# New list weights for the attention, a reordered start, and token gathers at another step of the ranked experts

## The chip, the core and the metric

The kernel runs on one core of a Trainium2 chip. The metric is the device time of one execution in microseconds (us). The core has a matrix engine (PE, whose weight loads are shown apart as PEld), a vector engine (DVE), an activation engine (ACT), a general engine (POOL) and a queue engine (SP) that only issues transfers. Each engine works through its own list of instructions in order; semaphores make one engine wait for another. Matrix products end up in PSUM banks; everything else lives in SBUF or in DRAM.

## The reference

Two stages follow each other. The first is causal attention with a decay, for 8 batches, 8 heads, 576 positions, head size 64:

```
scores = q k^T / 8 + cum[i] - cum[j],   cum = cumsum(log(clip(f, 1e-4, 1)))
attn   = softmax(scores, causal);       x = attn @ v      -> (8, 576, 512)
```

The second is a mixture of 8 experts with one expert for each token. A token takes the expert with the largest logit, or, where its local gate is at least 0.5, the expert of the token before it. Then

```
out[b, s] = p[e] * (relu(x[b, s] @ w1[e]) @ w2[e]),   w1: 512 x 1024, w2: 1024 x 512
```

The result has to be close to that of float32, so most operands are split into a high and a low half of 16 bits, and a product takes three matrix products of such halves.

## The kernel before, in words

**Attention (about 5 to 388 us of the span).** A batch is cut into 25 units of 512 score columns. A unit goes through these stages: scores on PE into a bank `st` (L905, with the mask added at L912), the negated row maximum on DVE (`nm`, L916), the exponential on ACT (`P`, L936), four transposes on PE into `pt` (L951), the high half on ACT (`ph`, L956), the low half on DVE (`pl`, L960), and the products with v on PE into `xp` (L930). For units named in `SUBS` the low half is made by PE and ACT in place of DVE (L963, L968). Beside that stand the turning of q and k for the next batch (L429, L438 to L442), the normalisation (L991, L995), and a side chain that computes the gate and the routing of earlier batches.

The order is written by a planner at build time. `issue()` keeps a clock for each engine and a queue for each stage, and takes the instruction with the smallest planned start plus a weight: `LEADS` has a weight for each stage and batch, `RANKS` settles ties, `SW` is the weight of the side chain, `GI` says after which unit a batch's gate is queued, `TS` and `TE` at which unit and on which engine (A for ACT, D for DVE) the turned groups of q and k are taken, `DUE` and `LATE` at which planned time the work of the first two batches is put in. The planned clock is not the chip's clock; the order it leaves is all that the chip sees.

**The start (`start()`).** Heads 0 to 2 of batch 0 are turned on PE (`heads`, L536) and get their decays by a small product with `spk` (`decays`, L541). `spk` comes from a chain: log on ACT (L278), a scan on DVE (L280), and casts and subtractions on DVE (`by_chunks`, `parts`, L287 to L300). `head_hi` and `head_b` (L554, L558) are ACT copies of a head, `head_lo` (L567, L569) is the low half on DVE.

**Experts (388 us to the end).** Experts 0 and 1 are done first; early parts of their tokens use `early_tok` (gathers by POOL at L1706, then transposes by SP at L1711). The other six are ranked by their number of tokens, rank r = 0 to 5. For each rank there are some 48 steps: steps 0 to 27 are `seven`, the first product by a scheme of seven half-size products (PE L1870, copies `et` on ACT at L1877, sums on DVE at L1883, relu on ACT L1887), and from step 28 on the second product `y`, four steps for each tile of 128 tokens (PE L1827, or L1831 for half a tile). A finished tile is scaled by ACT into `o` (L1763, L1798), and POOL writes it to its rows of the output (a scatter, L1766, L1799), behind a `drain` of POOL (L1773). There are three `o` buffers: the fourth `o` waits until the first one's scatter has landed.

What else a rank does is tied to its steps by a list, sorted by step: weight loads of the next rank by SP (four at step 0, one each at the steps in `UN` = 5, 24, 29), sums of weight quarters by POOL (`LA`, steps 6 to 13, L2154 to L2163), their halves by ACT and DVE (`WC`), and the tokens of rank r + 2: five gathers by POOL at step `XA[0]`, their transposes by SP at step `XA[1]`. A step is a place in the order, not a time: an instruction runs when its engine reaches it and its inputs are there.

Of the kernel before, what the change touches and what calls it, by code (L numbers as in the profile page):

```python
# [35 lines left out]
SUBS = ((7, 11, 14, 16), (7, 11, 14), (7, 11, 14, 16), (7, 11, 14, 16, 22), (7, 10, 11, 16), (7, 8, 11, 20), (2, 4, 11, 12, 14, 16), (7, 11, 13, 14, 21))  # L36


def moves_of(d):
# [17 lines left out]
GI = (21, 21, 16, 16, 16, 16, 11, 12)  # L57
SW = ((-700, 0, 0), (-700, 0, 0), (-700, 0, 0), (-700, 200, -200), (-700, 0, 0), (-700, 0, 0), (-700, 0, 0), (-800, 0, 0))
TS = ({'q': (13, 17, 18, 20, 20), 'k': (19, 20, 20, 21, 21)}, {'q': (13, 17, 18, 20, 20), 'k': (19, 20, 20, 21, 21)}, {'q': (13, 17, 18, 20, 20), 'k': (19, 20, 20, 21, 21)}, {'q': (13, 17, 18, 20, 20), 'k': (19, 20, 20, 21, 21)}, {'q': (13, 17, 18, 20, 20), 'k': (19, 20, 20, 21, 21)}, {'q': (13, 17, 18, 20, 20), 'k': (19, 20, 20, 21, 21)}, {'q': (13, 17, 18, 20, 22), 'k': (19, 20, 20, 21, 21)}, {'q': (12, 17, 18, 20, 20), 'k': (19, 20, 20, 21, 21)})
TE = ({'q': 'ADDDA', 'k': 'DAAAD'}, {'q': 'ADDDA', 'k': 'DAAAD'}, {'q': 'ADDDA', 'k': 'DAAAD'}, {'q': 'ADDDA', 'k': 'DAAAD'}, {'q': 'ADDDA', 'k': 'DAAAD'}, {'q': 'ADDDA', 'k': 'DAAAD'}, {'q': 'ADDDA', 'k': 'DAAAD'}, {'q': 'ADDDA', 'k': 'DAAAD'})  # L60
RANKS = (
# [8 lines left out]
)  # L70
LEADS = (
# [30 lines left out]
UC = (0, 0), (1, 1), (2, 2), (22, 23), (24, 25), (26, 27)  # L102
UB = 45
UN = (5, 24, 29)
XA = (32, 42)
# [11 lines left out]
def kernel(  # L117
# [138 lines left out]
    spm = cp.tile([64, 3, 512], F16, name="spm")  # L256
    spt = cp.tile([64, 3, 64], F16, name="spt")
    one = cp.tile([1, 1], F32, name="one")
    nc.vector.memset(one, 0.0)

    spk = cp.tile([97, 512], F16, name="spk")
    nc.vector.memset(spk, 0.0)
# [471 lines left out]
    def decays(h):  # L734
        for nm in "kq":
            add_decay(HS[h, nm], h, nm)
# [1939 lines left out]
```

## Time and profile before

| | |
|---|---|
| three runs | 777.99, 784.38 and 788.38 us; median 784.38 |
| profiled execution | 782.12 us, span of the instructions 780.3 us |
| PE busy | 733.5 us, 94% of the span |
| DVE, ACT, POOL busy | 598.4 (77%), 507.5 (65%), 467.3 us (60%) |
| DMA engines, mean busy share | 56.4% for the queue of SP's transfers, 8.1% for POOL's |
| granted PE clock | 1.00 in nearly all of the 40 slices, 0.995 on average |

The sums below are made against the profiled execution, which lies 2.3 us under the median of the three. PE's busy time counts each product up to a modelled end, so gaps of less than about 0.2 us between two products do not show as idle time. The idle time that an engine shows is followed by the name of what ended it, in square brackets.

### The profile page before, as it was taken

The page shows a single profiled execution, that of the slowest core. Times are in us where ns is not written, and L with a number is a line of the kernel's source. Part 1 is how long each engine was busy: PE and PEld are TensorE (multiplying, and loading weights), DVE is VectorE, ACT ScalarE, POOL GpSimd, SP SyncE. Part 2 cuts the span into 40 slices and gives each one's busy share as a digit, 9 for nine tenths or more (in the row PEclk, how much of TensorE's full clock was granted, in tenths as well). Part 3 has the DMA queues.
Part 4 walks back from the last instruction along what each step waited for, and adds up shares of the span by engine and source line. Part 5 has one row for each costly group of instructions (what it writes and reads, how often), then busy time and mean ns, then how long its engine had stood idle before and what let it go on. Part 6 is the DMA issues. An engine that isn't in the chain of part 4 may idle for free.

```text
span 780.3 us, 21918 instructions
## 1 busy us (share of the span) xinstructions
PE 733.5 (94%) x8661; PEld 533.4 (68%) x8661; DVE 598.4 (77%) x1295; ACT 507.5 (65%) x1006; POOL 467.3 (60%) x521
## 2 busy tenths in 40 slices
PE   5899999999999898988899999999999997999997
PEld 3687788788878777877655576675765655566683
DVE  7887788898998889899758847669596784868650
ACT  7898788888878878867643334456574644747441
POOL 5879989395689759838682464455371744434201
PEclk9999999999999999999999999999999998999999
DMA  7568979596976969156794766577658274651201
GB/s 177 146 132 176 167 181 187 132 194 162 182 175 128 178 162 179 38 102 197 179 272 149 221 138 142 149 210 162 212 139 233 78 161 181 169 206 56 82 3 51
DMA packets 189659, 120.75 MB, mean 155 GB/s; under 512 B 129397, under 2 KB 165511, under 8 KB 189532
## 3 DMA queue, kind: packets, MB, share of 16 engines
q1 hardware_dynamic: 183473, 100.19, 56.4%
q0 software_dynamic: 6080, 19.13, 8.1%
q8 instruction: 69, 1.13, 0.6%
q14 instruction: 37, 0.30, 0.1%
HBM read 72.25 MB, written 19.32 MB: 117 GB/s over the span
## 4 chain that ended last, share of the span: by engine, by line
PE 47%; issue 14%; DVE 10%; POOL 10%; POOLq 3%; DMA 3%; ACT 3%; SPq 0%; ACTq 0%; DVEq 0%
PE y L1827 9%; PE pt L951 7%; PE z L1785 6%; PE st L905 5%; PE xp L930 5%; PE zb L1870 5%; DVE nm L916 3%; POOLq L1773 3%; DVE pl L960 3%; POOL xg L1706 2%; PE st L429 2%; PE zd L1870 2%; DMA out_dram<-o,ranki 2%; POOL s L2163 2%; ACT ph L956 1%
## 5 line engine op out<-in xcount | busy, mean ns | idle before, releaser
L936 ACT ACTIVATE P<-st,nm 128x512 f32<-128x512 f32 (+3 forms) x288 | 152.4, 587 | 25.1 <-DVE nm L916 22.2
L956 ACT CAST ph<-pt 128x512 f16<-128x512 f32 (+1 forms) x200 | 115.0, 587 | 34.7 <-PE pt L951 31.9
L916 DVE TENSOR_REDUCE nm<-st 128x1 f32<-128x512 f32 (+4 forms) x264 | 133.1, 541 | 5.1 <-PE st L912 2.5
L960 DVE TENSOR_TENSOR pl<-pt,ph 128x512 f16<-128x512 f32 (+1 forms) x165 | 109.1, 669 | 22.8 <-ACT ph L956 21.0
L951 PE MATMUL pt<-ident,P 128*128 128x128 f32 x784 | 120.0, 278 | 6.0 <-DVE pl L960 3.3
L1766 POOL DMA_INDIRECT out_dram<-o,ranki x26 | 27.5, 1058 | 137.8 <-ACT o L1763 65.1
L951 PEld LDWEIGHTS pt<-ident,P 128*128 128x128 f32 x784 | 83.0, 141 | 22.3 <-DVE pl L960 5.0
L930 PE MATMUL xp<-VH,pl 128*128 128x65 f16 (+1 forms) x960 | 89.3, 194 | 6.6 <-DVE pl L960 5.9
L930 PE MATMUL xp<-VH,ph 128*128 128x65 f16 (+1 forms) x960 | 91.0, 195 | 2.0 <-ACT ph L956 2.0
L1827 PEld LDWEIGHTS <-hh 128*128 128x128 f16 x528 | 51.2, 98 | 58.6
L930 PE MATMUL xp<-VL,ph 128*128 128x65 f16 (+1 forms) x960 | 90.5, 194 | 0.0
L930 PEld LDWEIGHTS <-ph 128*128 128x128 f16 (+1 forms) x1920 | 83.1, 102 | 10.3 <-issue 3.1
L905 PE MATMUL st<-Ak,Aq 128*128 128x256 f16 (+4 forms) x448 | 77.0, 282 | 3.8 <-DVE den L1561 1.8
L930 PEld LDWEIGHTS <-pl 128*128 128x128 f16 (+1 forms) x960 | 74.7, 102 | 8.0 <-DVE pl L960 7.1
L905 PE MATMUL st<-KB,QB 70*128 70x256 f16 (+4 forms) x448 | 76.3, 278 | 0.0
L1827 PE MATMUL y<-ul,hh 128*128 128x512 f16 x168 | 63.8, 379 | 0.0
L1827 PE MATMUL y<-uh,hh 128*128 128x512 f16 x168 | 63.7, 379 | 0.0
L1827 PE MATMUL y<-uh,hl 128*128 128x512 f16 x168 | 63.7, 379 | 0.0
L1785 PE MATMUL z<-xT,wh 128*128 128x384 f16 (+2 forms) x256 | 55.0, 306 | 0.3 <-DVE hl L1749 0.2
L1827 PEld LDWEIGHTS <-hl 128*128 128x128 f16 x264 | 25.8, 98 | 30.8
L1763 ACT ACTIVATE o<-y,rank 128x512 f32<-128x512 f32 x23 | 15.7, 683 | 44.6 <-PE y L1827 25.7
L1870 PEld LDWEIGHTS <-wh 128*128 128x128 f16 x384 | 37.6, 98 | 9.2 <-issue 0.3
(441 smaller groups left out, 2013.8 us busy)
## 6 DMA issues: line engine op xcount, KB each, us to landing
stg<-in_moe_w_dram SPq DMA_DIRECT2D x64, 512.0 KB
xs<-xr SPq DMA_DIRECT2D x16, 512.0 KB
ldq<-in_q_dram SPq DMA_DIRECT2D x14, 512.0 KB
ldk<-in_k_dram SPq DMA_DIRECT2D x14, 512.0 KB
ldv<-in_v_dram SPq DMA_DIRECT2D x28, 256.0 KB
QB<-Aq SPq DMA_DIRECT2D x15, 256.0 KB
KB<-Ak SPq DMA_DIRECT2D x15, 256.0 KB
ldv<-in_v_dram SPq DMA_DIRECT2D x20, 64.0 KB
```

The source lines that it names most:

```text
L905: nc.tensor.matmul(st[p0:p0 + m, co:co + n], lhsT=queries(lq, kk, h, c), rhs=rhs, start=(ps == 0 and first and co == col), stop=(ps == 1), ...
L916: nc.vector.tensor_reduce(dst, src, axis=AX.X, op=ALU.max, negate=True)
L930: nc.tensor.matmul(xo, lhsT=a[:, c0:c0 + m], rhs=w[:, vi, :], start=False, stop=(i == n - 1 and jj == 2), skip_group_check=True)
L936: nc.scalar.activation(P[:, c0:c1].rearrange("p (k x r) -> p k r x", r=2, x=64), st[:, c0:c1].rearrange("p (k r x) -> p k r x", r=2, x=64) ...
L951: nc.tensor.matmul(U["pt"][:, i * 128:(i + 1) * 128], lhsT=P[:, i * 128:(i + 1) * 128], rhs=ident, is_transpose=True, start=(i == 0), stop ...
L956: nc.scalar.copy(U["ph"][:, :cols], U["pt"][:, :cols])
L960: nc.vector.tensor_tensor(U["pl"][:, :cols], U["pt"][:, :cols], U["ph"][:, :cols], ALU.subtract)
L1766: nc.gpsimd.indirect_dma_start(out=outf if EX.get("over") else next_out(), out_offset=bass.IndirectOffsetOnAxis(ap=scat(t)[0:m], axis=0), ...
L1773: nc.gpsimd.drain()
L1785: nc.tensor.matmul(z[:, a, 0:wd], lhsT=w[:, d, fc * 128:(fc + 1) * 128], rhs=xT[:, x, a * wd:(a + 1) * wd], start=(i == 0), stop=(i == len ...
L1827: nc.tensor.matmul(y[0:m], lhsT=a[:, fc, t * 128:t * 128 + m], rhs=u[:, fc], start=(i == 0), stop=(i == len(prods) - 1))
L1870: nc.tensor.matmul(out, lhsT=w, rhs=v, start=(start and i == 0), stop=(i == len(ops) - 1), skip_group_check=True)
```

## The change

**The planner's numbers.** `RANKS`, `LEADS`, `SUBS`, `GI`, `TS`, `TE`, `LATE` and `DUE` have new values. The lists of batches 1 and 2 come out nearly as they were; those of batches 0 and 3 to 7 differ. In all, 40 units in place of 35 have their low half made by PE and ACT: five L960 fewer on DVE, five L963 more on PE and five L968 more on ACT.

**The start.** The table of the log is loaded by a one-element log at the very beginning; a fill of `KB` is cut in two, and the second part comes behind the clip of f; the third cast in `parts` goes from DVE to POOL; head 2 is turned before the decays; the low halves of head 1 are put in by a due time of their own (`due_low`).

**The early tokens.** The gathers of expert 1's early tokens leave the side chain and stand behind the whole attention list (`early_tok(1)`).

**The ranked experts.** `XA` goes from (32, 42) to (6, 28), and the tile for the transposed tokens is made when the transposes are issued, since at step 6 both tiles are still in use. One `UC` step goes from 23 to 24.

```diff
-SUBS = ((7, 11, 14, 16), (7, 11, 14), (7, 11, 14, 16), (7, 11, 14, 16, 22), (7, 10, 11, 16), (7, 8, 11, 20), (2, 4, 11, 12, 14, 16), (7, 11, 13, 14, 21))
+SUBS = ((2, 7, 9, 14, 16, 24), (7, 11), (6, 11, 14, 16), (7, 11, 12, 22, 23), (9, 10, 11, 14, 16), (1, 6, 7, 8, 11, 13, 20, 22), (2, 4, 11, 12, 14, 16), (7, 12, 13, 14))
-GI = (21, 21, 16, 16, 16, 16, 11, 12)
+GI = (21, 21, 16, 17, 15, 16, 11, 17)
...
-    (-140, -60, -710, -30, -110, -210, -240, -440, -470, -130, -200, -90, -180, -50),
+    (-140, -60, -889, -184, -110, -301, -240, -615, -545, -131, -178, -101, -206, 167),
...
-UC = (0, 0), (1, 1), (2, 2), (22, 23), (24, 25), (26, 27)
+UC = (0, 0), (1, 1), (2, 2), (22, 24), (24, 25), (26, 27)
-XA = (32, 42)
+XA = (6, 28)
-LATE = ((12500, 'kh'), (13500, 'qh'), (15500, 'q2'), (15500, 'q3'), (17100, 'k2'), (17500, 'k3'), (22000, 'q4'), (23000, 'k4'))
-DUE = (('k2', 11500), ('q2', 12300), ('0', 12500), ('1', 20600), ('2', 25000), ('a', 27000), ('b', 29000), ('c0', 47000), ('c1', 56000))
+LATE = ((13890, 'kh'), (15975, 'qh'), (15500, 'q2'), (15244, 'q3'), (17250, 'k2'), (15221, 'k3'), (22093, 'q4'), (23000, 'k4'))
+DUE = (('l1', 10400), ('k2', 10991), ('q2', 12435), ('0', 12991), ('1', 20600), ('2', 24857), ('a', 27000), ('b', 28996), ('c0', 46469), ('c1', 56000))
...
-    nc.vector.memset(one, 0.0)
+    nc.vector.memset(one, 1.0)
...
-    nc.vector.memset(KB[0][64:70, 16:32], 1.0)
+    nc.scalar.activation(one, one, AF.Ln)
+    nc.vector.memset(KB[0][64:70, 16:26], 1.0)
...
     nc.vector.tensor_scalar(ft, ft, 1e-4, 1.0, ALU.max, ALU.min)
+    nc.vector.memset(KB[0][64:70, 26:32], 1.0)
...
-            nc.vector.tensor_copy(t[:, j], x)
+            if j == 2:
+                nc.gpsimd.tensor_copy(t[:, j], x)
+            else:
+                nc.vector.tensor_copy(t[:, j], x)
...
-        decays(0)
-        decays(1)
         heads(2)
-        decays(2)
-        for h in range(2):
-            for nm in "kq":
-                head_b(HS[h, nm], h, nm)
-                head_lo(HS[h, nm], h, nm)
+        for h in range(3):
+            decays(h)
+        for nm in "kq":
+            head_b(HS[0, nm], 0, nm)
+            head_lo(HS[0, nm], 0, nm)
+        for nm in "kq":
+            head_b(HS[1, nm], 1, nm)
...
+    def due_low():
+        for nm in "kq":
+            head_lo(HS[1, nm], 1, nm)
+        clock["DVE"] = T0 + 1898
...
-            nc.sync.dma_start_transpose(out=xT[:, :, i * 128:i * 128 + m], in_=xg[i][0:m])
+            nc.sync.dma_start_transpose(out=(xT() if callable(xT) else xT)[:, :, i * 128:i * 128 + m], in_=xg[i][0:m])
...
     issue()
+    early_tok(1)
...
-        xn = xp_.tile([128, 8, 608], F16, name="xT")
-        return xn, *token_steps(xp_, xn, lambda i: T.ranki[:, 0, r, i:i + 1], RANKC[r], bufs=XG)
+        xn = []
+
+        def tile():
+            if not xn:
+                xn.append(xp_.tile([128, 8, 608], F16, name="xT"))
+            return xn[0]
+
+        return tile, *token_steps(xp_, tile, lambda i: T.ranki[:, 0, r, i:i + 1], RANKC[r], bufs=XG)
```

Three places show how the order moves. The first is POOL in ranks 1 and 2: `out_dram` are the scatters of a rank's tiles, `stg` and `s` the sums of weight quarters, `xg` the gathers. Before, with the scatters of rank 1 at the top:

```order
L1766 DMA out_dram<-o,ranki 4608x512 x5
L2154 TENSOR_TENSOR stg<-stg 128x512
L2158 TENSOR_TENSOR s_12323<-stg 128x512
L2163 TENSOR_TENSOR s_12335<-stg,s_12323 128x512 x2
L2154 TENSOR_TENSOR stg<-stg 128x512
L2158 TENSOR_TENSOR s_12364<-stg 128x512
L2163 TENSOR_TENSOR s_12378<-stg,s_12364 128x512 x2
L1706 DMA xg<-xs,ranki 128x1024 x4
L1706 DMA xg<-xs,ranki 32x1024
L1766 DMA out_dram<-o,ranki 4608x512 x4
L1799 DMA out_dram<-o,hfi 9216x256
```

And with the change, at the same place:

```order
L1776 DMA out_dram<-o,ranki 4608x512 x5
L1716 DMA xg<-xs,ranki 128x1024 x4
L1716 DMA xg<-xs,ranki 32x1024
L2164 TENSOR_TENSOR stg<-stg 128x512
L2168 TENSOR_TENSOR s_12340<-stg 128x512
L2173 TENSOR_TENSOR s_12352<-stg,s_12340 128x512 x2
L2164 TENSOR_TENSOR stg<-stg 128x512
L2168 TENSOR_TENSOR s_12381<-stg 128x512
L2173 TENSOR_TENSOR s_12395<-stg,s_12381 128x512 x2
L1776 DMA out_dram<-o,ranki 4608x512 x4
L1809 DMA out_dram<-o,hfi 9216x256
```

The five gathers stood between the sums and a rank's scatters; now they stand ahead of the sums, and the scatters follow the sums directly.

The second place is PE in batch 0, at the first unit's transposes (`pt`) and its products with v (`xp`); `st<-ident` and `spk,pick` turn head 3. Before:

```order
L951 MATMUL pt<-ident,P 128x128 x4
L920 LDWEIGHTS eps
L920 MATMUL xp<-eps 128x2
L930 LDWEIGHTS ph
L930 MATMUL xp<-VH_112,ph 128x65
L930 LDWEIGHTS ph
L930 MATMUL xp<-VL_114,ph 128x65
L930 LDWEIGHTS pl
L930 MATMUL xp<-VH_112,pl 128x65
```

With the change:

```order
L961 MATMUL pt<-ident,P 128x128 x4
L541 MATMUL st<-ident,ldk 64x128 x4
L546 LDWEIGHTS pick
L546 MATMUL st<-spk,pick 6x512
L961 MATMUL pt<-ident,P 128x128 x4
L541 MATMUL st<-ident,ldq 64x128 x4
L546 LDWEIGHTS pick
L546 MATMUL st<-spk,pick 6x512
L961 MATMUL pt<-ident,P 128x128 x4
L434 LDWEIGHTS t16q
```

The products with v came directly behind their own transposes; now head 3, the transposes of two more units and a turned group of q stand between.

The third place is DVE in the start, from the last subtraction of `parts` to the first row maximum. Before:

```order
L300 TENSOR_TENSOR lg<-lg,spm 64x512
L295 CAST spk<-lg 4x512
L296 CAST spm<-lg 64x512
L569 TENSOR_TENSOR Ak<-st,Ak 64x512
L567 SCALAR_TENSOR_TENSOR Aq<-st,Aq 64x256 x2
L569 TENSOR_TENSOR Ak<-st,Ak 64x512
L567 SCALAR_TENSOR_TENSOR Aq<-st,Aq 64x256 x2
L916 TENSOR_REDUCE nm<-st 128x1
```

With the change:

```order
L305 TENSOR_TENSOR lg<-lg,spm 64x512
L297 CAST spk<-lg 4x512
L574 TENSOR_TENSOR Ak<-st,Ak 64x512
L572 SCALAR_TENSOR_TENSOR Aq<-st,Aq 64x256 x2
L574 TENSOR_TENSOR Ak<-st,Ak 64x512
L572 SCALAR_TENSOR_TENSOR Aq<-st,Aq 64x256 x2
L574 TENSOR_TENSOR Ak<-xp,Ak 64x512
L926 TENSOR_REDUCE nm<-st 128x1
```

The cast of 64x512 has left DVE (it stands on POOL ahead of `t16q`), and the subtraction of head 2 has come ahead of the first maximum.

## Rows read from the trace of the kernel before

**Rows 1.** Busy time of each engine by stages of the span; columns named in the head.

```profile
core 0: us, PE busy (x) PEld busy (x) DVE busy (x) ACT busy (x) POOL busy (x), PEclk, DMA share, GB/s
...
68.90:198.20 129.30, 126.65 (x2166) 106.36 (x2165) 112.11 (x262) 111.08 (x229) 101.52 (x129) 1.00 0.85 172
198.20:339.80 141.60, 132.16 (x2277) 111.33 (x2276) 125.17 (x315) 113.92 (x234) 108.17 (x127) 1.00 0.76 147
339.80:387.70 47.90, 40.38 (x723) 32.41 (x717) 43.41 (x108) 34.55 (x73) 30.97 (x30) 1.00 0.67 169
...
500.00:780.30 280.30, 266.38 (x2050) 175.22 (x2046) 185.43 (x305) 151.30 (x298) 111.76 (x91) 0.99 0.50 141
```

**Rows 2.** What PE waited for from 500 to 780: us, times, longest.

```profile
PE zb L1870 <- ACT et L1877: 7.8, 2, 6.2
```

**Rows 3.** Busy time in the 20 us around the longer of the two waits.

```profile
640.00:660.00 20.00, 13.79 (x113) 10.26 (x108) 6.92 (x15) 7.48 (x18) 7.49 (x7) 0.83 0.59 208
```

**Rows 4.** PE in order of time behind both waits: start, length, instruction, idle before.

```profile
598.56 0.28 PE L1870 MATMUL zb<-th,uh 128*128 128x288 f16 x1 [1.56 <-ACT et L1877]
...
600.39 0.29 PE L1870 MATMUL zb<-th,wh 128*128 128x288 f16 x1
...
649.11 0.40 PE L1870 MATMUL zb<-th,uh 128*128 128x288 f16 x1 [6.21 <-ACT et L1877]
...
652.67 0.30 PE L1870 MATMUL zb<-th,wh 128*128 128x288 f16 x1
```

**Rows 5.** ACT in order of time: before both waits, and a use of the sums.

```profile
597.53 0.69 ACT L1763 ACTIVATE o<-y,rank 128x512 f32<-128x512 f32 x1 [4.78 <-DMA out_dram<-o,ranki]
...
623.32 1.14 ACT L2119 ACTIVATE uh<-s 128x512 f16<-128x512 f32 x2
...
648.30 0.47 ACT L1798 ACTIVATE o<-y,hf 128x256 f32<-128x256 f32 x1 [6.81 <-DMA out_dram<-o,ranki]
```

**Rows 6.** POOL in order of time in rank 2.

```profile
622.75 1.92 POOL L1706 DMA_INDIRECT xg<-xs,ranki  x1
...
637.72 1.22 POOL L1766 DMA_INDIRECT out_dram<-o,ranki  x1 [6.24 <-ACT uh L2140]
641.67 1.00 POOL L1766 DMA_INDIRECT out_dram<-o,ranki  x1 [2.72 <-ACT o L1763]
```

**Rows 7.** Scatters from issue to landing in us: at 541, then at 641.67.

```profile
out_dram<-o,ranki POOLq DMA_INDIRECT x1, 2.8
...
out_dram<-o,ranki POOLq DMA_INDIRECT x1, 6.5
```

**Rows 8.** SP's queue in rank 2 in order of time.

```profile
627.22 10.60 SPq L1711 DMA_TRANSPOSE xT<-xg  x5
```

**Rows 9.** ACT at the start.

```profile
4.10 1.28 ACT L278 ACT_TABLE_LOAD   x1
```

**Rows 10.** DVE at the start.

```profile
2.34 1.76 DVE L264 MEMSET KB<- 6x2048 f16 x1 [0.46 <-issue]
...
9.00 0.42 DVE L296 CAST spm<-lg 64x512 f16<-64x512 f32 x1
...
11.72 2.22 DVE L296 CAST spm<-lg 64x512 f16<-64x512 f32 x1
```

**Rows 11.** POOL at the start.

```profile
11.50 2.17 POOL L725 TENSOR_TENSOR t16q<-ldq,t16q 128x1024 f16<-128x1024 f32 x1
```

**Rows 12.** PE at the start, in order of time.

```profile
11.84 1.86 PE L541 MATMUL st<-spk,pick 97*6 97x512 f16 x4 [3.04 <-DVE spk L295]
...
21.03 0.20 PE L930 MATMUL xp<-VH,ph 128*128 128x65 f16 x1 [0.67 <-ACT ph L956]
...
22.20 0.20 PE L930 MATMUL xp<-VH,pl 128*128 128x65 f16 x1 [0.93 <-DVE pl L960]
```

**Rows 13.** The early tokens: index on DVE, fourth gather on POOL, first use on PE.

```profile
372.73 0.17 DVE L1628 SCALAR_TENSOR_TENSOR xs<-xt,xe 128x9 int32<-128x9 f32 x1
...
381.31 0.96 POOL L1706 DMA_INDIRECT xg<-xs,xg  x1 [4.73 <-DMA xT<-xg]
...
387.71 0.50 PE L1785 MATMUL z<-xT,wh 128*128 128x384 f16 x2
```

More of the change, by code (lines that the diff above doesn't have):

```diff
@@ L54 @@
 XI = 3
-GI = (21, 21, 16, 16, 16, 16, 11, 12)
+GI = (21, 21, 16, 17, 15, 16, 11, 17)
 SW = ((-700, 0, 0), (-700, 0, 0), (-700, 0, 0), (-700, 200, -200), (-700, 0, 0), (-700, 0, 0), (-700, 0, 0), (-800, 0, 0))
-TS = ({'q': (13, 17, 18, 20, 20), 'k': (19, 20, 20, 21, 21)}, {'q': (13, 17, 18, 20, 20), 'k': (19, 20, 20, 21, 21)}, {'q': (13, 17, 18, 20, 20), 'k': (19, 20, 20, 21, 21)}, {'q': (13, 17, 18, 20, 20), 'k': (19, 20, 20, 21, 21)}, {'q': (13, 17, 18, 20, 20), 'k': (19, 20, 20, 21, 21)}, {'q': (13, 17, 18, 20, 20), 'k': (19, 20, 20, 21, 21)}, {'q': (13, 17, 18, 20, 22), 'k': (19, 20, 20, 21, 21)}, {'q': (12, 17, 18, 20, 20), 'k': (19, 20, 20, 21, 21)})
-TE = ({'q': 'ADDDA', 'k': 'DAAAD'}, {'q': 'ADDDA', 'k': 'DAAAD'}, {'q': 'ADDDA', 'k': 'DAAAD'}, {'q': 'ADDDA', 'k': 'DAAAD'}, {'q': 'ADDDA', 'k': 'DAAAD'}, {'q': 'ADDDA', 'k': 'DAAAD'}, {'q': 'ADDDA', 'k': 'DAAAD'}, {'q': 'ADDDA', 'k': 'DAAAD'})
+TS = ({'q': (13, 17, 18, 20, 20), 'k': (19, 20, 20, 21, 21)}, {'q': (13, 17, 18, 20, 20), 'k': (19, 20, 20, 21, 21)}, {'q': (13, 17, 18, 20, 20), 'k': (19, 20, 20, 21, 21)}, {'q': (13, 17, 18, 20, 20), 'k': (19, 19, 20, 21, 21)}, {'q': (13, 18, 18, 23, 20), 'k': (19, 20, 20, 20, 20)}, {'q': (13, 17, 18, 20, 20), 'k': (19, 20, 22, 22, 21)}, {'q': (13, 17, 18, 20, 22), 'k': (19, 20, 20, 20, 21)}, {'q': (10, 17, 18, 20, 20), 'k': (19, 20, 20, 21, 21)})
+TE = ({'q': 'ADDDA', 'k': 'DAAAD'}, {'q': 'ADDDA', 'k': 'DAADA'}, {'q': 'ADDDA', 'k': 'DAAAA'}, {'q': 'ADDDA', 'k': 'DAAAD'}, {'q': 'ADDDA', 'k': 'DAAAD'}, {'q': 'ADDDA', 'k': 'AAAAD'}, {'q': 'ADDDA', 'k': 'DADDD'}, {'q': 'ADDDA', 'k': 'DADAD'})
 RANKS = (
[8 rows of a table removed]
[8 rows of a table added]
 )
 LEADS = (
[8 rows of a table removed]
[8 rows of a table added]
 )
@@ L1168 @@
     now = [0]
-    clock = {"PE": T0, "ACT": T0 + 900, "DVE": T0 + 1300, "POOL": T0}
+    clock = {"PE": T0, "ACT": T0 + 900, "DVE": T0 + 300, "POOL": T0}
     due = deque()
@@ L1977 @@
     first_turns()
-    DO = {"k2": lambda: due_head("k"), "q2": lambda: due_head("q"), "0": due_0, "1": due_1, "2": due_2, "a": due_a, "b": due_b, "c0": lambda: due_c(0), "c1": lambda: due_c(1)}
+    DO = {"l1": due_low, "k2": lambda: due_head("k"), "q2": lambda: due_head("q"), "0": due_0, "1": due_1, "2": due_2, "a": due_a, "b": due_b, "c0": lambda: due_c(0), "c1": lambda: due_c(1)}
     due.extend((T, DO[f], ()) for f, T in DUE)
@@ L1987, in early_probs, with early_tok @@
         EX["p"] = probs(invp[:, :, 0:NE], NE, "x")
-    def early_tok():
-        for e in range(2):
-            xT = EX["xT", e] = ep.tile([128, 8, 128 * EARLY], F16, name=f"xT{e}")
-            tokens(ep, xT, lambda i: EX["g"][:, CAP * e + i:CAP * e + i + 1], 128 * EARLY, (B - 2) * S)
+    def early_tok(e=0):
+        xT = EX["xT", e] = ep.tile([128, 8, 128 * EARLY], F16, name=f"xT{e}")
+        tokens(ep, xT, lambda i: EX["g"][:, CAP * e + i:CAP * e + i + 1], 128 * EARLY, (B - 2) * S)
     for b in range(B):
@@ L2557 @@
     N.room(False)
-    xn = X0[0]
+    xn = X0[0]()
     N.x, parts_ = sums_of(xn, RANKC[0])
@@ L2570 @@
             N.x = None
-            xn = Xs[r + 1][0]
+            xn = Xs[r + 1][0]()
             todo += [call(0, N.load, ST)] + [call(x, N.load) for x in UN]
```

30 rows, old and new, of tables (LEADS, RANKS) are left out of this document.

## The prediction

> **What bounds the kernel now.** I read the windows by stage first, since PE is busy 94% of the span and the question is only where the other 6% lies. From 68.9 to 198.2 (batches 1 to 3) PE works 126.65 of 129.30 us, so 2.65 are idle, 2.05%; in batches 4 to 6 it is 141.60 - 132.16 = 9.44 us, 6.7%; in batch 7 47.90 - 40.38 = 7.52 us, 15.7%; in the ranked experts from 500 on 13.92 us [rows 1]. PE is the bound everywhere, and a change pays only where it removes PE's idle time or its work. DVE is the next engine: 125.17 of 141.60 us in batches 4 to 6 and 43.41 of 47.90 in batch 7, about 90%, against 87% in batches 1 to 3 [rows 1].
>
> Then the waits of PE from 500 on. Two idle stretches stand out: PE waited twice for an `et` copy of ACT, 7.8 us together [rows 2], 1.56 us at 598.56 and 6.21 us at 649.11 [rows 4]. Going back in order of time, ACT copied `et` late because an `o` ahead of it in its list waited 4.78 and 6.81 us for a scatter to land [rows 5]: all three `o` buffers were full. The scatters were late because POOL was. The first of rank 2 went out at 637.72 after 6.24 us in which POOL did nothing; the page names an ACT instruction, but SP had its last transpose of gathered tokens out at 627.22 + 10.60 = 637.82, and that transpose needs the last gather landed [rows 6, 8]. So I take it that POOL's `drain` ahead of the scatter held it until the gathers had landed; these began at 622.75, between sums and scatters. The second scatter, at 641.67, took 6.5 us to land where one at 541 took 2.8 [rows 6, 7], and 641.67 + 6.5 = 648.2 is when the `o` of the long wait could go [rows 5].
>
> There is a third loss behind the long wait. The mean granted clock in the 20 us around it is 0.83, with PE busy 13.79 us of them [rows 3]; PE had been idle for 6.21 us just before. From 649.11 to 652.67 are 15 steps of 288 columns in 3.56 us; the same from 598.56 to 600.39 take 1.83 [rows 4], which is about the ratio of the two clock levels, 1.2 and 2.4 GHz. So 1.73 us were lost to the lower level.
>
> **XA, the gathers at step 6 and the turns at step 28.** Nothing is added: in each rank that fetches tokens, the same five gathers and transposes move. The gathers leave the place ahead of the scatters, so the first scatter follows the sums, whose `o` has been waiting. In rank 2 that is a start at 632.4 at the latest, with the sums' end at 622.75 moved back by the whole time of five gathers (5 x 1.92 = 9.6 us at most [rows 6]), in place of 637.72: five us or more, against the waits of 4.78 and 6.81 us of `o` [rows 5]. Both waits of PE should go: 1.56 + 6.21 + 1.73 = 9.5 us. The low end is nothing, if scatters stay late for another reason; the high end is 9.5, as no other stall of PE hangs on this. Taken: **-9.5**, because the delay removed is about as long as the waits.
>
> What it costs: the five gathers, 1 to 2 us each on POOL (1.92 at 622.75 [rows 6]), now stand ahead of POOL's sums. POOL is busy 111.76 of 280.3 us [rows 1], so it has the room in sum, but the place matters: ACT takes the sums at 623.32, 0.6 us after the last of them ended at 622.75 [rows 5, 6]. The cover is that the previous rank's scatters, which stand ahead of the sums too, come earlier by those five us or more. On SP, five transposes (10.60 us in its list [rows 8]) move ahead of the weight load of step 29, which is needed only in the next rank: nothing. The gathers now run beside the next weights' loads on the DMA engines, whose share is 0.50 there [rows 1]; their tokens are for two ranks on: nothing.
>
> **The start.** The log waits for a table load of 1.28 us at 4.10 [rows 9], which goes to the beginning, where ACT waits for nothing but its one element (0.2 us): -1.1. The fill of `KB` (1.76 us for 2048 elements, so 0.66 for the 768 moved [rows 10]) and the clip behind it end before ACT is free for the log: nothing more. The cast of 2.22 us at 11.72 leaves DVE, and the subtractions behind it go up; POOL is to do it. PE waited 3.04 us for `spk` before the decays [rows 12], and head 2 is turned in that time now. Against this, head 2's subtraction (0.7 us) comes ahead of the first maximum. Between -1.1 and -1.1 - 2.22 = -3.3 I take -2.0, as other engines than DVE also stand ahead of the first maximum. The first products waited 0.67 and 0.93 us for the halves of their own unit [rows 12]; with other work in between that is -1.5 more (0 to -1.6). Sum **-3.5**, ends 0 and -4.9. Row first, rule behind: the same cast took 0.42 us at 9.00 and 2.22 at 11.72, where POOL's L725 ran beside it from 11.50 to 13.67 [rows 10, 11]. The Trainium skill, "SBUF — State Buffer", section "Who interferes with whom", says that the vector engine's two-port modes and GpSimd share one pair of ports as a lock held for the whole instruction, which agrees with these rows, and speaks against the move: POOL's cast would wait for, or hold up, a cast of DVE beside it. By that rule the term would be some 0.6 us smaller (an estimate).
>
> **The attention's lists.** Batches 1 and 2 stay. For 0 and 3 to 7 no row shows the new order, so I bound it by the batches that are there. If batches 4 to 7 sank to the 2.05% of batches 1 to 3, their 189.5 us would keep 3.9 of 16.96 us idle: -13.1. If batches 3 to 6 rose to batch 7's 15.7%, that is 141.60 x 0.157 - 9.44 = +12.8 and, for batch 3 (a third of 129.3 us), 43.1 x 0.137 = +5.9: +18.7. Within this the order gives signs. Five low halves go from DVE to PE and ACT, which helps the second engine and costs PE five small products. In batch 0 the first products no longer stand right behind their transposes; in batches 4 and 6 more do than before, in 7 as many. I take **-2**, near the row of today's own idle time, since better and worse places are mixed.
>
> **The early tokens.** Expert 1's gathers now follow the whole list. From the index at 372.73 to the fourth gather behind the first landed transpose at 381.31 are 8.6 us; to the first use at 387.71 15.0 [rows 13]. The index comes later in batch 7's new list, which cuts that cover to 9 to 11 us by what stands behind it. 0 to +3, taken 0. The `UC` step: nothing, one ACT copy a step later.
>
> **Sum**, against the profiled execution of 782.12 us, 2.3 under the median: -9.5 - 3.5 - 2 + 0 = -15, so **767**.
>
> **Rivals.**
> - *The lists gain too* (17%). Batches 4 to 7 come down to the idle share of batches 1 to 3: 782.1 - 9.5 - 3.5 - 13.1 = 756. For it: DVE near 90% there is relieved [rows 1]. Against: the order brings as many products close behind their transposes as before.
> - *POOL stays late* (17%). Gathers ahead of the sums push these back by up to 9.6 us, and the 0.6 us of cover at 623.32 is gone [rows 5, 6]. ACT's `o` stands behind that use, so the waits of PE stay, with another cause: the XA term is 0 and the time 782.1 - 5.5 = 776.6; if ACT lost 5 us in each of four ranks and PE felt it, up to 796. It decides at the point where the previous rank's scatters still end some 12 us into a rank. A second way to the same 776.6: the scatters land slowly beside the transposes, as at 641.67 [rows 7] beside weight loads. The Trainium skill, "DMA: Bandwidth & Descriptors", section "Queues, rings and completion order", says that a DMA engine takes turns between its queues a packet at a time, which agrees with the 6.5 us against 2.8.
> - *The lists lose* (10%), the other side. Units of batches 3 to 6 wait for DVE's maxima and low halves as those of batch 7 do now: 782.1 + 18.7 - 9.5 - 3.5 = 788. It decides with the place of the products: once most of them stand right behind their own transposes, PE idles for every unit. For it: batches 4 and 6 have more such units; against: fewer low halves on DVE.
> - *The change doesn't do what it says* (6%). The turned tokens need a tile that the running rank still reads until step 27; if SP's transposes wait for it and hold the weight loads behind them, a rank begins late. Batch 7's tokens coming late at its end lies here too: 767 + 3 to 767 + 9.5, so 770 to 777.
>
> **Chances and range.** My forecast has 50%, within 764 to 772. A measurement of this kernel tells about 2% from no change: 768.7 and 800.1 around the median of 784.4. Faster: the first rival (17) and a little over two thirds of the forecast (36), 53%. Slower than 800: a part of the lost lists and the late sums, 7%. The rest, 40%, within. Range 756 to 781: it leaves out half of the first rival, and the lost lists.
>
> **What would show it.** XA: POOL's order gathers, sums, scatters without idle time ahead of the first scatter, `o` never waiting for `out_dram` by more than a us, no PE wait for `et` over 1 us, and the granted clock at 1.00 all through the ranks. Start: log near 4.3, first maximum 1 to 3 us earlier than before, batch 1 beginning 3 to 4 us earlier. Lists: idle of PE by batch, 16.96 us in batches 4 to 7 now, about 15 then. It is wrong if PE waits for ACT in the ranks with `uh<-s` as the late one, if the idle share of batches 4 to 7 passes 11%, or if PE waits for `xT` at the end of the attention.

## The result: slower by 1%, and the profile after

Ten runs of the changed kernel have a median of 787.87 us (784.79 to 791.90). Ten of the kernel before, with the three shown above, have 779.10 (776.92 to 788.38); its profiled execution of 782.12 us lies above that. The ratio is 1.0104, with a 95% interval of 1.0077 to 1.0131. Ratios, here and below, compare only executions in the faster of two states and aren't quotients of the medians, which are over all. The forecast was 767, faster. The profiled execution of the changed kernel took 786.62 us, span 784.8.

These are the windows by stage of the changed kernel, with the columns of [rows 1]: batches 1 to 3, 4 and 5, 6, 7, and the span from 500 on.

```profile
core 0: us, PE busy (x) PEld busy (x) DVE busy (x) ACT busy (x) POOL busy (x), PEclk, DMA share, GB/s
65.30:195.00 129.70, 127.24 (x2192) 107.21 (x2190) 112.17 (x261) 112.13 (x230) 102.20 (x129) 1.00 0.81 171
195.00:287.70 92.70, 88.83 (x1488) 73.93 (x1485) 82.81 (x207) 76.50 (x158) 67.49 (x82) 1.00 0.77 155
287.70:336.70 49.00, 46.54 (x821) 39.08 (x818) 43.17 (x101) 37.35 (x78) 40.08 (x47) 0.97 0.65 123
336.70:387.90 51.20, 43.51 (x667) 34.53 (x665) 45.88 (x112) 34.23 (x73) 30.68 (x29) 0.93 0.63 150
500.00:784.80 284.80, 269.73 (x2063) 177.01 (x2061) 184.48 (x307) 154.13 (x302) 110.27 (x92) 0.98 0.48 140
```

Batch 1 begins 3.6 us earlier (65.3 for 68.9), yet the first product of expert 0 comes at 387.9, as before (387.7), and rank 0 begins at 505.1 instead of 502.4. Batches 6 and 7 show a mean granted clock of 0.97 and 0.93, where [rows 1] have 1.00. From 500 on PE is idle for 15.07 us against 13.92. From rank 0 to the end it takes 279.7 us against 277.9.

The waits of PE from 500 on, in the changed kernel (us, times, longest):

```profile
PE zb L1880 <- ACT et L1887: 7.3, 3, 4.7
PE zb L1880 <- issue: 1.5, 1, 1.5
```

So PE waits for `et` as long as in [rows 2], but at another place and for another reason. No `o` waits for a scatter any more: the waits of [rows 5] for `out_dram` have no row after. Instead, in rank 0, PE in order of time:

```profile
515.81 0.29 PE L1880 MATMUL yt<-xT,wl 128*128 128x304 f16 x1
520.82 0.41 PE L1880 MATMUL zb<-th,wh 128*128 128x304 f16 x1 [4.71 <-ACT et L1887]
```

ACT at the same time:

```profile
513.93 0.42 ACT L1897 ACTIVATE hh<-zd 128x304 f16<-128x304 f32 x1 [0.93 <-DVE zd L1893]
520.35 0.73 ACT L1887 COPY et<-zb 128x304 f32<-128x304 f32 x2 [6.00 <-remote]
```

POOL at the same time:

```profile
512.79 0.98 POOL L1716 DMA_INDIRECT xg<-xs,ranki  x1 [0.30 <-issue]
514.08 0.97 POOL L1716 DMA_INDIRECT xg<-xs,ranki  x1 [0.30 <-issue]
515.35 0.95 POOL L1716 DMA_INDIRECT xg<-xs,ranki  x1 [0.30 <-issue]
516.61 0.95 POOL L1716 DMA_INDIRECT xg<-xs,ranki  x1 [0.31 <-issue]
517.86 0.90 POOL L1716 DMA_INDIRECT xg<-xs,ranki  x1 [0.30 <-issue]
523.44 1.25 POOL L2164 TENSOR_TENSOR stg<-stg 128x512 f32<-128x512 f32 x1 [4.68 <-DMA stg<-in_moe_w_dram]
```

And the chain of waits of the changed kernel there (start, us, what):

```profile
513.93 0.42 ACT hh L1897
514.36 5.92 another core or an unknown queue
520.28 0.02 issue
```

The products of PE that the two `et` copies need were over at 514.55 and 515.33, yet the copies began only at 520.35. The page finds no instruction that released ACT then. The semaphore records of the trace say what did: PE's updates by the products that end at 514.55, 515.33 and 516.10 stand at 520.28, 520.36 and 520.43, in one burst, 1.5 us after POOL's last gather has ended, and ACT's wait for that semaphore ends at 520.31.

Such records have to be counted with care, because some are missing altogether. PE's update at 513.00 has none, and yet DVE's sum that waits for it runs at 513.43, so it came in time. I call an update **late** when it has a record of its own that comes over 0.5 us after the instruction that raises it has ended, and **missing** when no record is left for it. "Beside" a gather is from its start to 1.5 us behind its end. Of PE's 763 updates away from any transfer of POOL none is late or missing; of 25 beside the ranked gathers 17 are late, by up to 5.7 us, and 2 are missing. Of ACT's and DVE's none is late anywhere; 13 of 21 and 12 of 23 beside the ranked gathers are missing, which tells nothing on when they came. In the profile of before PE has 11 updates beside the ranked gathers and 788 away from POOL's transfers, and none of them is late or missing.

The expectations below were written with a looser count, the next record of the semaphore, under which a missing record passes for a late update: the 7.3 us in them is the update at 513.00. The counts outside of the expectations are by the definition above.

The granted clock falls to the lower of its two levels for 3.41 or 6.83 us at some places where PE idles. In rank 0 the fall comes inside the wait of 4.71 us, as in the long wait of before [rows 3, 4]. The changed kernel, around batch 6's fall and in rank 0:

```profile
290.00:296.50 6.50, 4.04 (x67) 2.92 (x66) 6.50 (x12) 3.72 (x10) 6.32 (x7) 1.00 1.09 187
296.50:299.90 3.40, 3.40 (x23) 2.75 (x22) 2.84 (x10) 2.58 (x6) 3.32 (x6) 0.50 1.31 170
515.00:525.00 10.00, 5.29 (x26) 3.14 (x25) 1.94 (x5) 2.31 (x6) 4.32 (x6) 0.67 0.94 303
```

It fell four times ahead of the last products: at 296.5, 361.4, 381.9 (3.4 us each) and 518.4 (6.8 us). In the 6.9 us before the second and the third of these PE was idle for 1.45 and 2.92 us. In the first profile of before it fell once ahead of the last products, at 645.9.

### The profile page after: what moved, and what is told of

Its sections match the earlier page's. It is cut to its first block, busy times and chain, and to the rows that moved or that the text cites. A ratio compares the mean times of both kernels' runs of the same rounds, so it can differ in the third digit from the quotient of the medians.

```text
span 784.8 us, 21928 instructions
## 1 busy us (share of the span) xinstructions
PE 739.4 (94%) x8666; PEld 538.0 (69%) x8666; DVE 595.5 (76%) x1291; ACT 507.6 (65%) x1010; POOL 466.5 (59%) x522
## 4 chain that ended last, share of the span: by engine, by line
PE 65%; DVE 13%; issue 9%; ACT 4%; POOL 2%; DMA 2%; POOLq 2%; SPq 1%; another core or an unknown queue 1%; ACTq 0%; DVEq 0%
PE y L1837 14%; PE pt L961 9%; PE st L915 8%; PE xp L940 7%; PE z L1795 7%; PE zb L1880 6%; DVE nm L926 3%; PE st L434 3%; PE zd L1880 3%; DVE pl L970 2%; PE yt L1880 2%; ACT ph L966 1%; POOLq L1783 1%; ACT P L946 1%; PE st L922 1%
## 5 line engine op out<-in xcount | busy, mean ns | idle before, releaser
L961 PE MATMUL pt<-ident,P 128*128 128x128 f32 x784 | 122.8, 281 | 4.6 <-ACT Ak L443 0.9
L970 DVE TENSOR_TENSOR pl<-pt,ph 128x512 f16<-128x512 f32 (+1 forms) x160 | 106.4, 671 | 21.4 <-ACT ph L966 20.0
L1776 POOL DMA_INDIRECT out_dram<-o,ranki x26 | 34.2, 1316 | 141.0 <-ACT o L1773 96.1
L1887 ACT COPY et<-zb 128x288 f32<-128x288 f32 (+4 forms) x72 | 27.9, 393 | 26.4 <-PE zb L1880 17.3
## 6 DMA issues: line engine op xcount, KB each, us to landing
stg<-in_moe_w_dram SPq DMA_DIRECT2D x64, 512.0 KB
xs<-xr SPq DMA_DIRECT2D x16, 512.0 KB
ldq<-in_q_dram SPq DMA_DIRECT2D x14, 512.0 KB
ldk<-in_k_dram SPq DMA_DIRECT2D x14, 512.0 KB
```

Source lines behind the costliest of these rows:

```text
L961: nc.tensor.matmul(U["pt"][:, i * 128:(i + 1) * 128], lhsT=P[:, i * 128:(i + 1) * 128], rhs=ident, is_transpose=True, start=(i == 0), stop ...
L970: nc.vector.tensor_tensor(U["pl"][:, :cols], U["pt"][:, :cols], U["ph"][:, :cols], ALU.subtract)
L1776: nc.gpsimd.indirect_dma_start(out=outf if EX.get("over") else next_out(), out_offset=bass.IndirectOffsetOnAxis(ap=scat(t)[0:m], axis=0), ...
L1887: nc.scalar.copy(t, x)
```

## The experiments

Each was timed against the kernel before in five rounds on one chip. There were three chips, so medians compare well only with that of before beside them; all are in the table behind the experiments.

**XA alone.** The kernel before with

```diff
-XA = (32, 42)
+XA = (6, 28)
```

and the tile made late.

> The kernel before with the gathers at step 6 and the turns at step 28 alone; start, lists and early tokens as before. Theory S (signals): in the changed kernel's trace semaphore updates of PE came up to 7.3 us late in the 4 to 6 us in which POOL issues five gathers beside the short products of `seven`, and in the kernel before none came later than 0.45 us; the move itself does it, so this kernel loses 1 to 5 us in each of four ranks, gains back the waits for full `o` buffers, and ends 2 to 9 us above the kernel before (median 779), with late updates at ranks 0 to 3. Theory P (the prediction's own step): the two waits of PE go, -5 to -9.5 us, 770 to 774, and no late updates. Theory L (lists): the loss is in the attention, so this kernel is like P.

Ratio 1.0049 (1.0012 to 1.0086), 786.25 us: slower, by about 4 us. No `o` waits for `out_dram` in its profile, and 15 of 28 updates of PE beside the ranked gathers are late, by up to 3.4 us. PE's waits from 500 on, in a profiled execution of 781.13 us, one of its fastest:

```profile
PE zb L1870 <- ACT et L1877: 4.7, 4, 2.0
PE zb L1870 <- issue: 1.1, 2, 0.7
```

S holds, the prediction's step falls: its waits go, and others come.

**All but XA.** The changed kernel with the same line turned back.

> The changed kernel with XA back at (32, 42). Theory S: the ranks are as before (about 277 us from the first rank's start), the start's 3.6 us stay gained; if only the ranks' gathers make the late updates, 776 to 780, and late updates remain only at the early tokens' gathers, where they cost about 4 us at the end of the attention. Theory L: as the changed kernel or worse, 786 to 795, since the lists lose and the ranks lose nothing. Theory P: 9.5 us above the changed kernel, 797.

781.34 us, ratio 1.0020 (0.9993 to 1.0047). PE's longest wait from 500 on is 0.7 us, for an `o` that waited 4.9 us for a scatter:

```profile
PE y L1832 <- issue: 2.4, 6, 0.5
PE y L1841 <- ACT o L1773: 0.7, 1, 0.7
```

None of the 10 updates of PE beside the ranked gathers is late. So XA costs the changed kernel about 0.8%, 6.5 us (an estimate from the two ratios, whose intervals leave 3.5 to 9.5), and all the rest together comes out near nothing. The profiles agree: from rank 0 to the end it is 273.7 us here and 279.7 in the changed kernel. L and the prediction's own step are ruled out for XA.

**The lists alone.** The kernel before with the planner's numbers of batches 1 to 7 of the change.

```diff
-SUBS = ((7, 11, 14, 16), (7, 11, 14), ...
+SUBS = ((7, 11, 14, 16), (7, 11), (6, 11, 14, 16), ...
```

(and so `GI`, `TS`, `TE`, `RANKS`, `LEADS`).

> The kernel before with the planner's numbers of batches 1 to 7 alone; start, batch 0, early tokens and XA as before. Theory L: batches 6 and 7 take 1.8 and 3.3 us longer as in the changed kernel's trace, batches 4 and 5 0.7 and 1.0 less, so 3 to 5 us above the kernel before: 782 to 784. Theory S: the 1.9 us wait of PE at 377 in the changed kernel and the lower clock of batches 6 and 7 came from late updates beside gathers, not from the order, so with no late updates the lists are within 2 us of the kernel before, 777 to 781.

792.26 us, ratio 1.0165: both theories miss. With the old start these numbers lose 11 us up to expert 0 (398.8 for 387.7).

**The lists undone.** The changed kernel with the old numbers of batches 1 to 7.

> The changed kernel with the planner's numbers of batches 1 to 7 as before (start, batch 0, early tokens behind the list and XA changed). Theory L: 3 to 5 us under the changed kernel's 788, so 783 to 785. Theory S: still 784 to 789, with late updates in the windows of the ranks' gathers.

785.28 us, ratio 1.0053 (1.0016 to 1.0091), with 16 of 27 updates of PE late beside the ranked gathers. Both expectations overlap here, so this tells little; but its expert 0 begins at 390.2, later than the changed kernel's 387.9. From batch 1 to expert 0 take 318.8 us with old start and old numbers, 331.5 with the old start and new numbers, 326.3 with new start and old numbers, 322.6 with both new. By these profiles the new numbers lose 12.7 us with the old start and win 3.7 with the new one. The loss shows in the time too (1.0165), the win doesn't: the ratio with the old numbers, 1.0053, is not above the changed kernel's 1.0104.

**The kernel before again**, for a second profile.

> The kernel before, unchanged, for a second profile. Its first profile is the only one of six without late semaphore updates beside gathers (none later than 0.45 us). Theory S1: late updates belong to gathers and not to the changed code, and the first profile was an exception; then updates up to 2 to 5 us late stand beside the gathers here too, with the ranks' gathers beside the second product, where PE waits for ACT seldom, so that PE's waits for ACT from 500 on stay under 1 us apart from waits for full `o` buffers. Theory S2: they come from what the changed kernels share; then none here.

781.91 us. In the ranks S2 holds and not S1: of PE's 11 updates beside the ranked gathers none is late and 2 are missing. In the whole profile 3 are late, by 0.7 us at most, all beside other gathers. What sets the first profile apart is that hardly a record is missing in it (1 of PE's, none of ACT's and 1 of DVE's, against 8, 24 and 27 here). The delays up to 5.3 us that the looser count gives here are missing records in the second product, where PE raises an update every 5.2 us. So at the old place of the gathers the kernel before has no late update in either profile. Of the one wait of PE over 1 us, 3.8 us for `et` at 645, the reason is the prediction's, since `o` waits (us, times, longest):

```profile
ACT o L1798 <- DMA out_dram<-o,ranki: 6.2, 1, 6.2
ACT o L1763 <- DMA out_dram<-o,ranki: 2.8, 1, 2.8
```

**Plain loads.** In the changed kernel the gathers of ranks 2 to 5 are

```diff
-            nc.gpsimd.indirect_dma_start(out=t[0:m], out_offset=None, in_=xs[0:rows], ...
+            nc.sync.dma_start(out=t[0:m], in_=xs[128 * i:128 * i + m])
```

> The changed kernel with the five gathers of ranks 2 to 5 replaced by five plain transfers of SP's queue at the same step (the first rows of the tokens in place of the ranked ones, so the output of those experts belongs to other tokens); bytes and places are the same, but POOL makes no addresses. Theory S (POOL's work on a gather holds up the other engines' updates): no late updates in ranks 0 to 3, the waits of PE for `et` there go (7.3 + 1.5 us in the changed profile and the lower clock behind them), 4 to 9 us under the changed kernel: 779 to 784. Rival D (the transfer beside the weight loads on the DMA engines does it): late updates and waits stay, 786 to 790.

776.73 us (774.92 to 778.65), ratio 0.9931 (0.9897 to 0.9965). In its windows and its waits of PE from 500 on:

```profile
500.00:776.00 276.00, 268.43 (x2071) 176.89 (x2068) 184.35 (x310) 155.00 (x302) 92.46 (x75) 1.00 0.49 146
...
PE y L1835 <- DVE hl L1901: 0.5, 1, 0.5
PE y L1844 <- ACT o L1776: 0.4, 1, 0.4
```

The wait for `et` is gone, the clock doesn't fall in the ranks ahead of the last products, and PE is idle for 6.9 us (the span ends at 775.3) instead of 15.07. D is ruled out: as many bytes beside the weight loads don't do it. The edit takes three things away at once, though: POOL's work on the addresses, the scattered rows (these are consecutive ones) and POOL's own queue. Which of them holds the updates up isn't shown. It is 2 us under what S expected.

**The gathers alone.** `XA = (6, 42)` in the changed kernel.

> The changed kernel with XA = (6, 42): gathers early, turns where they were. Theory S: as the changed kernel, 786 to 790, since the gathers' place does it. Rival Q (the transposes at step 28 ahead of a weight load on SP's queue): as with (32, 42), 780 to 783.

791.15 us, ratio 1.0132 (1.0068 to 1.0195), with 17 of 26 updates late: the gathers' place does it; Q falls.

**The early tokens in the chain again.**

```diff
-    early_tok(1)
```

(and both experts' tokens back in the side chain).

> The changed kernel with the early tokens of expert 1 back in the side chain. Theory S: its three gathers at 386.9 to 390.4 delayed the last updates of the attention by up to 3.4 us and PE's first transposes of the last tokens with them (1.7 us at 392.6); with the gathers earlier, 2 to 3 us under the changed kernel, 785 to 786. Rival (the place of the early tokens hangs on nothing, as predicted): the same as the changed kernel, 787 to 788.5.

790.01 us, ratio 1.0097: the rival's no-change, and S misses. PE's wait of 1.7 us for the last tokens is gone, but 1.1 us for the transposed last rows stand in its place.

**A spread train.** The five gathers singly between POOL's sums.

```diff
-XA = (6, 28)
+XA = ((6.5, 8.5, 10.5, 12.5, 13.5), 28)
```

> The changed kernel with the five gathers of a rank not in one train but singly between POOL's sums (ahead of step 6, 8, 10, 12, 13); turns at step 28 as in the changed kernel. The gathers still stand beside `seven`, and POOL makes the same addresses. Theory T (a train does it: the late updates begin with the third to fifth gather of a train and end as the train's transfers land, so something fills up): no update over 0.5 us late in ranks 0 to 3, PE's waits for `et` there under 1 us in sum, 777 to 782. Rival G (every gather holds up the updates for its own time): late updates of up to 1 us at each of the 19 gathers, 784 to 789.

783.71 us, ratio 1.0022 (0.9992 to 1.0052), between the two. None of the 40 updates of PE beside the ranked gathers is late (4 are missing), PE doesn't wait for `et` at all, and from the start of rank 0's first product to that of the last one it is 266.0 us instead of 273.5. Its waits of PE over 1 us from 500 on are others:

```profile
PE y L1837 <- DVE wl L2152: 3.4, 2, 2.8
PE y L1841 <- ACT o L1773: 2.2, 1, 2.2
```

So with 3.5 us from one gather to the next in place of 1.3 the late updates are gone, as T has it, though the gathers still stand beside `seven` and POOL makes the same addresses; G falls. The time misses T's range all the same: `wl`, a half of the next weights, now comes late, and rank 0 begins at 512.0 instead of 505.1, for reasons that I didn't trace beyond the 2.2 us for `o` and a fall of the clock at 509.3.

**Spread in the second product.**

```diff
-XA = (6, 28)
+XA = ((28, 32, 37, 42, 43), 45)
```

> The changed kernel with a rank's gathers in the second product, two ahead of the first scatter and three behind it (steps 28 to 43, turns at 45). There PE needs ACT once in 4.8 us. Theory S: late updates cost little there, the first scatter waits for two gathers' landing only, 778 to 783, under the 781 of the changed kernel with XA (32, 42) if the full `o` buffers cost something there. Rival: the turns at step 45 and the loads behind them on SP come late, a rank's first products or sums wait, 785 or more.

777.50 us, ratio 0.9954 (0.9930 to 0.9978): faster than both kernels. POOL in rank 1 of this kernel:

```profile
580.69 1.26 POOL L1716 DMA_INDIRECT xg<-xs,ranki  x1
582.26 0.96 POOL L1716 DMA_INDIRECT xg<-xs,ranki  x1 [0.30 <-issue]
587.13 1.29 POOL L1776 DMA_INDIRECT out_dram<-o,ranki  x1 [3.91 <-ACT th L1961]
588.73 1.40 POOL L1716 DMA_INDIRECT xg<-xs,ranki  x1 [0.30 <-issue]
```

The first scatter goes at 587.13, behind two gathers; before it stood behind five and waited 6.24 us [rows 6]. No `o` waits for `out_dram`, and 1 of 11 updates is late, by 1.2 us; PE's waits for `et` sum to 0.5 us.

**Old numbers for batches 6 and 7**, new ones for the rest, XA (32, 42).

> The changed kernel with XA (32, 42) and the planner's numbers of batches 6 and 7 as before. In six kernels with the new numbers the granted clock fell to 0.50 for 3.4 us (or 6.8) at about 296, 361 and 382, which at half speed is 1.7 us of PE's work each; in the kernels with the old numbers of those batches at most once. Theory C (the lists of batches 6 and 7 cost 4 to 5 us, by these falls): batches 6 and 7 together 95 to 97 us instead of 100 to 102, 3 to 5 us under the changed kernel with XA (32, 42), 776 to 778. Rival (the old numbers of 6 and 7 don't fit the new start and batches 1 to 5, as the undone lists showed: 99.9 us for both batches): 780 to 783.

784.87 us, ratio 1.0045 (1.0007 to 1.0084): C falls. Its batches 6 and 7:

```profile
287.90:338.30 50.40, 45.45 (x762) 37.60 (x759) 41.97 (x101) 38.55 (x80) 40.69 (x46) 1.00 0.65 127
338.30:387.80 49.50, 41.78 (x732) 33.21 (x730) 44.71 (x112) 34.77 (x73) 31.01 (x30) 1.00 0.56 149
```

The clock doesn't fall here, which C was right about, but the two take 99.9 us all the same, with more idle time in place of the slow products.

**The early tokens by plain loads.** As above, for the six early gathers.

> The changed kernel with the six gathers of the early tokens (at 375 to 379 and 387 to 390) replaced by plain transfers of SP's queue (fixed rows, so the early outputs belong to other tokens); XA = (6, 28) as in the changed kernel. Theory S (late updates beside these gathers cost the end of the attention 1.9 us at 377 and the last tokens 1.7 us at 392): both waits go, batch 7 takes 48 to 49 us instead of 51, 3 to 4 us under the changed kernel: 783.5 to 785. Rival (batch 7 is longer by its list's own order): batch 7 stays at 51 to 53 us, 786 to 788.

788.35 us, ratio 1.0134. At the place, S is right; batch 7 of this kernel:

```profile
336.40:385.10 48.70, 42.37 (x667) 33.53 (x666) 45.36 (x112) 34.16 (x73) 27.83 (x27) 0.96 0.65 159
```

It is 2.5 us shorter and expert 0 begins at 385.1. But the plain loads and their transposes take turns on SP's queue up to 401.8, a weight load behind them lands only at 407.9, and PE waits 4.2 us for the routing at 409: this edit brought a loss of its own, and its total says nothing on S.

**The best place in the kernel before.** Old start, lists and early tokens with the spread of the second product.

> The kernel before (its start, lists and early tokens) with the ranks' gathers as in the spread version of the second product (steps 28 to 43, turns at 45). With the changed kernel's start and lists this measured 777.5 (ranks 263.1 us in the profile instead of 271). Attention and experts 0 and 1 of the kernel before end 2.5 to 5 us earlier than the changed kernel's (502.5 against 505 to 508). Theory: the two add up, 772 to 775. Rival (the start's and lists' difference in profiles is chance): 777 to 778.

775.92 us (771.24 to 781.78), ratio 0.9945 (0.9911 to 0.9978). It beats both kernels, but not the same spread with the new start and lists by more than the intervals tell; the sum of 772 to 775 isn't shown.

| kernel | median, us | before beside it, us | ratio to before |
|---|---|---|---|
| changed | 787.87 | 779.10 | 1.0104 |
| XA alone | 786.25 | 780.41 | 1.0049 |
| all but XA | 781.34 | 780.41 | 1.0020 |
| lists alone | 792.26 | 780.41 | 1.0165 |
| lists undone | 785.28 | 780.41 | 1.0053 |
| plain ranked loads | 776.73 | 783.04 | 0.9931 |
| gathers alone | 791.15 | 783.04 | 1.0132 |
| early tokens in the chain | 790.01 | 783.04 | 1.0097 |
| spread between the sums | 783.71 | 781.86 | 1.0022 |
| spread in the second product | 777.50 | 781.86 | 0.9954 |
| old numbers for 6 and 7 | 784.87 | 781.86 | 1.0045 |
| plain early loads | 788.35 | 781.21 | 1.0134 |
| before, spread in the second product | 775.92 | 781.21 | 0.9945 |

## Why the prediction was wrong, step by step

**XA, -9.5: this step failed**, and with it the sign. Its mechanism was right: with the gathers out of the scatters' way the waits of `o` for `out_dram` went in every kernel that moved or replaced them, and stayed (4.7 to 16 us in sum) in those with (32, 42). Two things were wrong. The size: the first profile of before had PE wait 7.8 us [rows 2]; its second has 3.8, and all but XA less than 1 (that kernel has the new `UC` step too, which no run tries by itself). I took one execution's stall, with the clock's loss behind it, for the kernel's. And the price: "five gathers, 1 to 2 us each on POOL ... it has the room in sum", and beside the next weights' loads "nothing". I charged the gathers only to POOL and the DMA engines. What they cost falls on PE's updates, which come late beside them, and so on ACT, which waits for these, and on PE, which waits for ACT. In `seven` PE raises an update about every 0.8 us and soon needs ACT's answer: in the six kernels with five gathers in a train at step 6, 24 to 30 updates stand beside the ranked gathers, and 14 to 17 of them are late. At the old place, beside the second product with its update every 5.2 us, it is 7 to 11, and none of the 49 in five profiles is late (3 are missing). And of 40 beside single gathers in `seven` none is late either (4 are missing): it takes the train and the place. Measured: about +6.5 us (all but XA against the changed kernel) or +4 (XA alone against before), where -9.5 stood. No row of the first profile showed it, since not one update there was late; but the bound said "The low end is nothing, if scatters stay late for another reason; the high end is 9.5, as no other stall of PE hangs on this", and nothing excluded a loss from putting a step beside another kind of work. The rival that POOL stays late named the right effect (waits of PE for ACT stay with another cause) and even let the time rise to 796, but by the wrong way: `uh<-s` is nowhere what PE waits for.

**The start, -3.5: right in its sum.** Batch 1 begins 3.6 us earlier. Batch 0's new list numbers are in this too; no run parts them from the start. The log and the first maximum, of the changed kernel, ACT, DVE and POOL:

```profile
4.38 0.68 ACT L280 ACTIVATE lg<-ft 64x576 f32<-64x576 f32 x1
...
9.65 0.42 DVE L297 CAST spk<-lg 4x512 f16<-4x512 f32 x1
...
15.07 0.67 DVE L926 TENSOR_REDUCE nm<-st 128x1 f32<-128x512 f32 x1
...
9.76 0.78 POOL L299 CAST spm<-lg 64x512 f16<-64x512 f32 x1 [4.75 <-DVE lg L305]
```

The log at 4.38 (4.3 was forecast), the maximum 2.5 us earlier than 17.60; in two other profiles of the old start it comes at 16.0 and 16.8, so 1 to 2.5 us is what the start wins there. PE's waits for `ph` and `pl` up to batch 1 went from 2.9 to 0.5 us, more than the 1.5 of the sum, but waits for other inputs took their place, so that only the sum is shown to be right and not each of its terms. No row shows the 0.6 us that the Trainium skill's rule ("SBUF — State Buffer", "Who interferes with whom") would have taken away: POOL's cast took 0.78 us here with DVE's small cast of 0.42 beside it, and no DVE cast met a longer instruction of POOL any more, where the same cast on DVE had taken 2.22 beside L725 [rows 10, 11].

**The lists, -2: wrong in sign, and the wrong quantity.** I bounded them by PE's idle time. That did fall: 14.02 us in batches 4 to 7 (3.87, 2.46 and 7.69 of the windows above) against 16.96, about the forecast 15. But the time rose from 189.5 to 192.9 us, since PE's busy time rose from 172.5 to 178.9. The three falls of the clock make 3 x 1.7 = 5.1 us of that; the remaining 1.2 us are near what four more products L973 in these batches cost at 0.38 us each, though no run parts them. All eight kernels with the new numbers of batches 6 and 7 and the new start show these three falls; with the old numbers there is none or one in these batches, and in the kernel with old numbers for 6 and 7 more idle time. Why it falls there and not in the kernel before, where PE idled for 2.79 of the 7 us from 294 to 301 and the clock stayed at 1.00, these runs don't show. The 3.6 us of the start are given back here, since from batch 1 to expert 0 it takes 322.6 us instead of 318.8. With the old numbers it would be 326.3, by one profile whose kernel isn't slower in total.

**The early tokens, 0 (0 to +3).** From the first product of expert 0 to rank 0 it is 117.2 us instead of 114.7; 1.7 us of this is PE's wait for the last tokens at 392. But with the gathers back in the chain it is 117.0. So the 2.5 us are there, inside the range, and their cause stays open.

**The sum.** -9.5 - 3.5 - 2 + 0 stood against about +6.5 for XA and, by the ratio of 1.0020, about +1.6 for all the rest, which isn't clear of nothing. The measured time lies at the rival of the lost lists, 788, which the range left out, but that is luck: its cause, more idle time in the lists, didn't come. No rival charged XA with a loss of its own beyond POOL's lateness.

## What to carry to other kernels

Ask of a moved step not only whether its engine and its queue have room, but what the other engines do at the new place: here gathers by POOL did best beside long products with slack, in twos and threes (0.9954 and 0.9945), and worst as a train beside a chain of short answers between PE and ACT. A stall in one profile is one draw: look at a second before it becomes a term. Idle time isn't the whole price of an order, since the clock can make the busy time longer; and numbers that a planner was given for one start may lose under another, as these did under the old one.

## What the runs showed of the hardware

Beside a train of five gathers by POOL, 1.3 us from one to the next, the semaphore updates of PE's short products come late by 0.5 to 5.7 us, in the changed kernel often in a burst 1.1 to 1.5 us behind the train's end: 14 to 17 of 24 to 30 in six kernels, the changed one among them with 17 of 25. Single gathers 3.5 us apart at the same place do this to none of 40, trains beside the long products of the second product to none of 49. Away from POOL's transfers none of some 750 to 790 updates is late in any of the 15 profiles. In the attention of the changed kernel all 5 updates beside the early tokens' gathers are late too, by up to 3.4 us. Plain loads of the same bytes by SP don't do it. Of ACT's and DVE's updates no late record shows; beside the gathers many have no record at all.

What inside the chip holds the updates back wasn't tried: POOL's work on the addresses, the scattered rows and POOL's queue are all still open. Nor was it tried whether the recording has a part in it. Every execution here comes with a span and a granted clock of its own, so none shows what the gathers cost when nothing is recorded.
